# Output projection of a recurrent-attention block: eight block products against seven, on one core

## The chip, the core and the metric

The kernel runs on one core of a Trainium2 chip. The core has five engines that run side by side, each with a queue of its own: TensorE (PE in the profile; PEld is its weight load) multiplies matrices and writes its results into PSUM, VectorE (DVE) and ScalarE (ACT) do element by element work and can read PSUM, GpSimd (POOL) works on SBUF alone, and SyncE (SP) issues the DMAs. PSUM has eight banks of 512 float32 columns by 128 partitions.

The metric is the time of one execution in device microseconds. The kernel before takes 991.49 us (median of 3 runs, 991.46 to 991.51).

## The reference

There are B = 8 batches, H = 8 heads of D = 64, S = 512 tokens and Ns = 32 states in each batch. Tokens attend to states and states to tokens; the results are put one behind the other and go through a gated feed-forward block:

```python
scores = scale * np.matmul(x, state.transpose(0, 1, 3, 2))
a = softmax(scores)
xread = np.matmul(a, state)                      # (8, 8, 512, 64)
scores2 = scale * np.matmul(state, x.transpose(0, 1, 3, 2))
a2 = softmax(scores2)
sread = np.matmul(a2, x)                         # (8, 8, 32, 64)
x = concat([xread, sread]) -> (4352 tokens, 512)
xn = x / sqrt(mean(x * x) + 1e-06) * rms_g
g = xn @ w_gate                                  # 512 x 1536
val = xn @ w_val                                 # 512 x 1536
out = (g * sigmoid(g) * val) @ w_out             # 1536 x 512
```

(softmax and concat stand for the lines written out in the reference.) The feed-forward weights arrive as float64; the output is float32, 4352 x 512. The last line, the product with w_out, is what the change is about.

## The kernel before, in words

All matmuls are float32. One matmul of the source is two MATMUL instructions and two weight loads (LDWEIGHTS) in the trace. The stationary operand (lhsT) is 128 x 128, the moving operand (rhs) up to 512 columns wide.

*Start.* The weights are converted from float64 to float32 piece by piece on VectorE, GpSimd and ScalarE (lines 134 to 157): 24 pieces of w_gate and w_val into the tile w, 12 of w_out into the tile wo, in the order in which they are needed. The attention of batches 0 and 1 runs beside it.

*Batch loop* (lines 398 to 423). Batch b has two stages.

The **hidden stage** goes over m = 0 to 11, the twelve blocks of 128 of the 1536 hidden features. For every second m, make_v (lines 329 to 342) multiplies the states with the gate and value weights into v, which needs eight small matmuls (16 instructions, L335) and two ScalarE copies (L342). hidden (lines 344 to 360) then makes two 128 x 512 products in two PSUM banks, gp for the gate and vp for the value (two matmuls each, L350), and ScalarE takes a tanh of gp (L355). Two VectorE instructions make the hidden value h (L356, L358), 128 features by 512 tokens, in SBUF, from a pool of 14 buffers. Behind every m, between() puts two steps of the attention of batch b + 2 into the instruction stream, so that these are used up after the tenth m; in the projection between() has nothing left to issue, but in batch 0, where conversions may be left.

The **projection** (project, lines 362 to 372) goes over four blocks r of 128 tokens. For each it sums twelve matmuls, h of block m by wo of block m, 512 columns wide, in one PSUM bank (L367); ScalarE copies the bank to SBUF (L370) and SP issues the store of 128 x 512 (L377). make_v for the next batch's first two blocks stands right ahead of the projection.

*End.* Behind batch 7 the 256 state tokens of all batches go through the same two stages: hidden with w itself as the stationary operand and 256 columns (four matmuls per product, 192 instructions in all), and a projection of two blocks of 128 (48 instructions), each stored by four DMAs (L383).

PSUM: the pool fps has four banks and serves gp, vp and the projection (tile name f), in turn; aps and vps have two banks each, for the attention and for make_v. A bank comes free when its last reader is done.

The source gives the work in an order, but the framework fixes each engine's instruction order when it is built, by the source's order and by estimated times of what is ready, and places the semaphore waits.

Of the kernel before, what the change touches and what calls it, by code (L numbers as in the profile page):

```python
# [8 lines left out]
F32 = mybir.dt.float32  # L9
I32 = mybir.dt.int32  # L10
U32 = mybir.dt.uint32
ALU = mybir.AluOpType
# [4 lines left out]
P = 128  # L17
RAW_AHEAD = 4
# [4 lines left out]
def kernel(  # L23
# [103 lines left out]
    def ready(n):  # L127

        nonlocal n_ready
        while n_ready < min(n, len(pieces)):  # L130
            to_float32(n_ready)
            n_ready += 1

    def to_float32(k):


        load_piece(k + RAW_AHEAD)
        if k not in raw:
# [5 lines left out]
        top = two.tile([P, NI, P], I32, name="top")  # L144
        ex = two.tile([P, NI, P], I32, name="ex")
        man = two.tile([P, NI, P], F32, name="man")
# [14 lines left out]
    aT_s = {}  # L161
    xsT = consts.tile([P, NI, NT], F32, name="xsT")
# [146 lines left out]
    def state_norm():  # L309

        sq = one.tile([P, NI, NT], F32, name="sqT", tag="eS")
        SE.activation(out=sq, in_=xsT, func=ACTF.Square)
        sp = aps.tile([P, NT // P], F32, name="at")
        for r in range(NT // P):
            for i in range(NI):
                TE.matmul(out=sp[:, r:r + 1], lhsT=sq[:, i, P * r:P * r + P], rhs=ones[:, 0:1],
                          start=(i == 0), stop=(i == NI - 1))
        ss = two.tile([P, NT // P], F32, name="sst")
        VE.tensor_copy(ss, sp)
        rp = along(inverse_rms(ss, NT // P), NT // P)  # L320
# [8 lines left out]
    def make_v(b, mp):  # L329

        ready(4 * mp + 4)
        pv = [vps.tile([P, 4 * P], F32, name="pv") for e in range(2)]
        for j in range(4):
            for e in range(2):
                TE.matmul(out=pv[e][Ns * j:Ns * j + Ns, :],  # L335
                          lhsT=stT_g[b][D * e:D * e + D, j, :],
                          rhs=w[D * e:D * e + D, j, 2 * mp:2 * mp + 2].rearrange(
                              "p m k f -> p (m k f)"),
                          start=True, stop=True)
        v = v_sb[b, mp] = two.tile([P, 2, 2, 2, P], F32, name="v")  # L340
        for e in range(2):
            SE.copy(v[:, e].rearrange("p m k f -> p (m k f)"), pv[e])  # L342

    def hidden(m, n, lhs, rhs):

        gp = fps.tile([P, S], F32, name="f")
        vp = fps.tile([P, S], F32, name="f")
        for k, ps in enumerate((gp, vp)):
            for i, r in enumerate(rhs):
                TE.matmul(out=ps[:, 0:n], lhsT=lhs(i, k), rhs=r,  # L350
                          start=(i == 0), stop=(i == len(rhs) - 1))
        t = three.tile([P, S], F32, name="t", tag="t")
        h = hpool.tile([P, S], F32, name="h")

        SE.activation(out=t[:, 0:n], in_=gp[:, 0:n], func=ACTF.Tanh, scale=0.5)  # L355
        VE.scalar_tensor_tensor(out=t[:, 0:n], in0=t[:, 0:n], scalar=1.0, in1=gp[:, 0:n],  # L356
                                op0=ALU.add, op1=ALU.mult)
        VE.scalar_tensor_tensor(out=h[:, 0:n], in0=t[:, 0:n], scalar=0.5, in1=vp[:, 0:n],  # L358
                                op0=ALU.mult, op1=ALU.mult)
        return h  # L360

    def project(hh, n, store, between):
        ready(len(pieces))
        for r in range(n // P):
            op = fps.tile([P, DM], F32, name="f")
            for m in range(NM):
                TE.matmul(out=op, lhsT=hh[m][:, P * r:P * r + P], rhs=wo[:, m, :],  # L367
                          start=(m == 0), stop=(m == NM - 1))
            ot = three.tile([P, DM], F32, name="ot", tag="t")
            SE.copy(ot, op)  # L370
            store(r, ot)
            between()

    def store_tokens(b):
        def store(r, ot):
            r0 = T * b + P * r
            nc.sync.dma_start(out=out[r0:r0 + P, :], in_=ot)  # L377
        return store

    def store_states(r, ot):  # L380
        for j in range(4):
            r0 = T * (4 * r + j) + S
            nc.sync.dma_start(out=out[r0:r0 + Ns, :], in_=ot[Ns * j:Ns * j + Ns, :])  # L383

    done = object()
    for k in range(RAW_AHEAD):
        load_piece(k)
    load_state(1)
# [9 lines left out]
    for b in range(B):  # L398
        if b + LOOKAHEAD < B:
            steps = attention(b + LOOKAHEAD)  # L400
        elif b + LOOKAHEAD == B:
            steps = state_norm()
        else:
            steps = iter(())

        def between():
            for _ in range(2):
                next(steps, done)
                ready(n_ready + 1)

        hh = []
        for m in range(NM):
            if m % 2 == 0 and m + 2 < NM:
                make_v(b, m // 2 + 1)
            v = v_sb[b, m // 2]
            hh.append(hidden(m, S, lambda e, k: v[:, e, m % 2, k, :],
                             [aT_s[b][:, e, :] for e in range(2)]))
# [39 lines left out]
```

## Time and profile before

| what | value |
|---|---|
| median of 3 runs | 991.49 us |
| the profiled execution | 991.61 us |
| its span, first to last instruction | 989.6 us |
| mean granted TensorE clock | 0.971 |
| TensorE (PE) busy | 915.4 us, 3682 instructions |
| VectorE busy | 345.1 us |
| ScalarE busy | 226.3 us |
| GpSimd busy | 135.1 us |
| the projections' matmuls (L367) | 352.4 us, 816 instructions |
| the token hidden stages' matmuls (L350) | 357.6 us, 768 instructions |
| the states' hidden matmuls (L350) | 41.6 us, 192 instructions |

Engines overlap, so their busy times don't add up to the span. In a group of instructions, "busy" is the time in which at least one of the group runs, and the mean is that of one from start to end; TensorE starts an instruction before the one ahead of it has ended, so the mean of a matmul is longer than the distance between two of them. Times in a timeline or in the chain are microseconds from the start of the span. An arrow <- behind an idle time names what the engine waited for. "issue" is time in which an engine waited for nothing that the profile shows.

### The profile page before, as it was taken

To read this page: it belongs to the slowest core of one execution; us is meant where nothing else is said; L and a number is where in the kernel's file an instruction comes from. 1 tells how busy PE (TensorE), PEld (TensorE's weight loads), DVE (VectorE), ACT (ScalarE), POOL (GpSimd) and SP (SyncE) were. 2 spreads that over 40 slices of the span, in tenths; PEclk is the share of its full clock that TensorE was granted. 3 is DMA by queue.
4 is the path that set the end of the run, shared out by engine and by line. 5 is a ranking of instruction groups with operands and counts; after the bars stand their busy time and mean duration, and the time that the engine had idled before them with its cause. 6 is when DMAs were issued, how large, how long until landed. Compare 5 with 4: busy or idle time off the path is not lost.

```text
span 989.6 us, 9226 instructions
## 1 busy us (share of the span) xinstructions
PE 915.4 (93%) x3682; PEld 427.7 (43%) x3682; DVE 345.1 (35%) x533; ACT 226.3 (23%) x436; POOL 135.1 (14%) x169
## 2 busy tenths in 40 slices
PE   3487666999999999999999999999999999999998
PEld 2233323444444444444544454444444344344783
DVE  4899899402530153015300530054103300320120
ACT  3334233102420242014201430143102201210110
POOL 4766776100000000000000000001000000000000
PEclk9987787999999999999999999999999999999999
DMA  7463532200020002000200000000000000000000
GB/s 183 149 171 113 156 116 76 43 32 14 1 46 22 25 0 46 21 25 1 45 22 22 1 1 11 32 1 1 11 22 11 1 22 21 1 0 32 11 1 21
DMA packets 58363, 37.83 MB, mean 38 GB/s; under 512 B 40144, under 2 KB 52432, under 8 KB 58320
## 3 DMA queue, kind: packets, MB, share of 16 engines
q1 hardware_dynamic: 58320, 37.24, 13.2%
q8 instruction: 29, 0.48, 0.2%
q14 instruction: 14, 0.11, 0.0%
HBM read 28.31 MB, written 8.91 MB: 38 GB/s over the span
## 4 chain that ended last, share of the span: by engine, by line
PE 81%; DVE 10%; POOL 4%; issue 3%; SPq 1%; DMA 1%; ACT 0%; POOLq 0%; DVEq 0%
PE f L367 36%; PE f L350 35%; PE pv L335 4%; DVE ex L155 2%; PE at L271 2%; DVE top L152 2%; DVE man L153 2%; DVE ex L147 1%; POOL ex L150 1%; PE at L198 1%; POOL ex L149 1%; PE at L209 1%; PE at L177 1%; PE at L296 1%; DVE h L358 1%
## 5 line engine op out<-in xcount | busy, mean ns | idle before, releaser
L350 PE MATMUL f<-aT_s,v 128*128 128x512 f32 x768 | 357.6, 608 | 5.0 <-DVE t L356 4.4
L367 PE MATMUL f<-wo,h 128*128 128x512 f32 x816 | 352.4, 593 | 0.0
L356 DVE SCALAR_TENSOR_TENSOR t<-t,f 128x512 f32<-128x512 f32 (+1 forms) x108 | 70.9, 656 | 513.8 <-ACT t L355 513.8
L367 PEld LDWEIGHTS f<-wo,h 128*128 128x128 f32 x816 | 154.5, 190 | 197.3 <-issue 191.3
L350 PEld LDWEIGHTS f<-aT_s,v 128*128 128x128 f32 x768 | 140.2, 192 | 183.8 <-issue 152.1
L355 ACT ACTIVATE t<-f 128x512 f32<-128x512 f32 (+1 forms) x108 | 61.8, 572 | 201.4 <-PE f L350 189.7
L370 ACT COPY ot<-f 128x512 f32<-128x512 f32 x34 | 19.9, 586 | 331.8 <-PE f L367 331.8
L358 DVE SCALAR_TENSOR_TENSOR h<-t,f 128x512 f32<-128x512 f32 (+1 forms) x108 | 70.7, 654 | 47.4 <-PE f L350 47.1
L335 PE MATMUL pv<-w,stT_g 64*32 64x512 f32 x768 | 60.8, 609 | 9.2 <-POOL w L157 8.4
L342 ACT COPY v<-pv 128x512 f32<-128x512 f32 x96 | 51.7, 588 | 60.2 <-PE pv L335 59.8
L221 POOL TENSOR_SCALAR m<-m 128x2 f32<-128x2 f32 x8 | 2.8, 356 | 374.8 <-DVE m L218 374.8
L350 PE MATMUL f<-xsT,w 128*128 128x256 f32 x192 | 41.6, 379 | 0.0
L151 ACT ACTIVATE man<-raw 128x512 f32<-128x512 uint32 x36 | 24.5, 681 | 73.3 <-POOL w L157 44.9
L350 PEld LDWEIGHTS f<-xsT,w 128*128 128x128 f32 x192 | 36.5, 190 | 5.4 <-issue 0.5
L155 DVE SCALAR_TENSOR_TENSOR ex<-raw,ex 128x512 int32<-128x512 int32 x36 | 34.9, 969 | 5.9 <-POOL ex L150 5.9
L271 PE MATMUL at<-bd,aT 128*128 128x256 f32 x128 | 33.9, 410 | 1.4 <-ACT aT L263 0.7
L157 POOL TENSOR_TENSOR w<-man,ex 128x512 f32<-128x512 f32 x24 | 32.2, 1344 | 18.3 <-DVE ex L155 15.4
L271 PEld LDWEIGHTS at<-bd,aT 128*128 128x128 f32 x128 | 25.5, 204 | 15.2 <-issue 4.8
L149 POOL TENSOR_SCALAR ex<-ex 128x512 int32<-128x512 int32 x36 | 27.7, 769 | 24.5 <-DVE ex L147 23.4
L147 DVE TENSOR_SCALAR ex<-raw 128x512 int32<-128x512 int32 x36 | 28.9, 804 | 2.3 <-POOL w L157 2.3
L177 PE MATMUL at<-dg,ones 128*128 128x512 f32 (+1 forms) x18 | 12.0, 757 | 19.0 <-POOL dg L174 19.0
L153 DVE SCALAR_TENSOR_TENSOR man<-top,man 128x512 f32<-128x512 int32 x36 | 28.7, 798 | 0.4
(66 smaller groups left out, 442.0 us busy)
## 6 DMA issues: line engine op xcount, KB each, us to landing
x_b<-in_x_dram SPq DMA_DIRECT2D x32, 256.0 KB, 4.5
out_dram<-ot SPq DMA_DIRECT2D x32, 256.0 KB, 2.0
raw<-in_moe_w_gate_dram SPq DMA_DIRECT2D x12, 512.0 KB, 3.7
raw<-in_moe_w_val_dram SPq DMA_DIRECT2D x12, 512.0 KB, 3.6
raw<-in_moe_w_out_dram SPq DMA_DIRECT2D x12, 512.0 KB, 3.3
rows<-in_state_dram SPq DMA_DIRECT2D x32, 16.0 KB, 2.0
bd<-in_state_dram SPq DMA_DIRECT2D x32, 16.0 KB, 1.7
out_dram<-ot SPq DMA_DIRECT2D x8, 64.0 KB, 1.7
```

Source lines behind the costliest of these rows:

```text
L147: VE.tensor_scalar(ex, hi, 20, 0x7ff, op0=ALU.logical_shift_right, op1=ALU.bitwise_and)
L149: GE.tensor_scalar(ex, ex, 1151.0, 896.0, op0=ALU.min, op1=ALU.max)
L153: VE.scalar_tensor_tensor(out=man, in0=top, scalar=2.0 ** -20, in1=man, op0=ALU.mult, op1=ALU.add)
L155: VE.scalar_tensor_tensor(out=ex, in0=hi, scalar=-(1 << 31), in1=ex, op0=ALU.bitwise_and, op1=ALU.bitwise_or)
L271: TE.matmul(out=rp[:, e, :], lhsT=aT[:, e, c, :], rhs=bd[:, e].rearrange("p j d -> p (j d)"), start=True, stop=True)
L335: TE.matmul(out=pv[e][Ns * j:Ns * j + Ns, :], lhsT=stT_g[b][D * e:D * e + D, j, :], rhs=w[D * e:D * e + D, j, 2 * mp:2 * mp + 2].rearrange ...
L342: SE.copy(v[:, e].rearrange("p m k f -> p (m k f)"), pv[e])
L350: TE.matmul(out=ps[:, 0:n], lhsT=lhs(i, k), rhs=r, start=(i == 0), stop=(i == len(rhs) - 1))
L355: SE.activation(out=t[:, 0:n], in_=gp[:, 0:n], func=ACTF.Tanh, scale=0.5)
L356: VE.scalar_tensor_tensor(out=t[:, 0:n], in0=t[:, 0:n], scalar=1.0, in1=gp[:, 0:n], op0=ALU.add, op1=ALU.mult)
L358: VE.scalar_tensor_tensor(out=h[:, 0:n], in0=t[:, 0:n], scalar=0.5, in1=vp[:, 0:n], op0=ALU.mult, op1=ALU.mult)
L367: TE.matmul(out=op, lhsT=hh[m][:, P * r:P * r + P], rhs=wo[:, m, :], start=(m == 0), stop=(m == NM - 1))
```

## The change

The product with w_out is made by halves. For the tokens of a batch (n = 512, and n = 256 for the states) the hidden values h form a matrix of two token halves by two feature halves A(i, j) (i the token half, j the half of the twelve blocks m), and wo one of two feature halves by two output halves B(i, j). Instead of the eight products of half blocks, seven are made (the scheme of Strassen and Winograd), from sums of blocks:

- The hidden values are in one tile hb, 128 x 12 x 512, in place of the pool of 14 buffers. In batches 1 to 7 and for the states, hidden adds two VectorE instructions for m = 6 to 11: the sum s of two quarters of the hidden values (128 x 256) and a difference that overwrites the lower token half of block m - 6.
- weight_sums makes three matrices of weight sums (t1, t2, t4) and overwrites one quarter of wo, in twelve VectorE instructions of 128 x 512. They are put behind the first three m of batch 1.
- project_seven makes the seven products, each of R x 6 matmuls with 256 columns (R = 2 blocks of 128 rows, 1 for the states), in three banks: zs, xs and ys, each holding both row blocks side by side. Products 2, 3, 4 and 7 go into xs and products 1 and 6 into zs without clearing it in between, so that PSUM keeps the partial sums; product 5 goes into ys. In between, keep copies the sums so far to SBUF on ScalarE (p5 from zs, p1 and u2 and at the end c21 from xs), s is overwritten twice on VectorE (two instructions of 128 x 768 each time), and finish adds a kept copy to a bank on VectorE and stores the result as 128 x 256.
- Batch 0 keeps project as it was. Behind it the pools of the conversion (raws, and conv for its three intermediates) are closed, and the new tiles are put into their place.

```diff
-    raws = ctx.enter_context(tc.tile_pool(name="raws", bufs=RAW_AHEAD))
-    hpool = ctx.enter_context(tc.tile_pool(name="hpool", bufs=NM + 2))
...
+    early = ExitStack()
+    raws = early.enter_context(tc.tile_pool(name="raws", bufs=RAW_AHEAD))
+    conv = early.enter_context(tc.tile_pool(name="conv", bufs=2))
...
+    hb = consts.tile([P, NM, S], F32, name="hb")
...
-        h = hpool.tile([P, S], F32, name="h")
+        h = hb[:, m, :]
...
+        if seven and m >= HM:
+            k = m - HM
+            upper, lower = hb[:, k, 0:n // 2], hb[:, k, n // 2:n]
+            VE.tensor_tensor(out=seven["s"][:, k, 0:n // 2], in0=lower, in1=hb[:, m, n // 2:n],
+                             op=ALU.add)
+            VE.tensor_tensor(out=lower, in0=upper, in1=lower, op=ALU.subtract)
...
+    def weight_sums():
+        late = ctx.enter_context(tc.tile_pool(name="late", bufs=1))
+        seven["pool"] = ctx.enter_context(tc.tile_pool(name="halves", bufs=7))
+        seven["t"] = late.tile([P, 3, HM, HD], F32, name="wt")
+        seven["s"] = late.tile([P, HM, S // 2], F32, name="hs")
+        t1, t2, t4 = (seven["t"][:, i] for i in range(3))
+        for k in range(0, HM, 2):
+            def blk(i, j):
+                return wo[:, HM * i + k:HM * i + k + 2, HD * j:HD * j + HD]
+            for dst, a, b in ((t1[:, k:k + 2], blk(0, 1), blk(0, 0)),
+                              (t2[:, k:k + 2], blk(1, 1), t1[:, k:k + 2]),
+                              (blk(0, 1), blk(1, 1), blk(0, 1)),
+                              (t4[:, k:k + 2], blk(1, 0), t2[:, k:k + 2])):
+                VE.tensor_tensor(out=dst, in0=a, in1=b, op=ALU.subtract)
+            yield
+
+    def project_seven(n, store, between):
+        half = n // 2
+        R = half // P
+        t, s, pool = seven["t"], seven["s"], seven["pool"]
+        def product(ps, lhs, rhs, start):
+            for r in range(R):
+                for k in range(HM):
+                    TE.matmul(out=ps[:, r, :], lhsT=lhs(k)[:, P * r:P * r + P], rhs=rhs(k),
+                              start=(start and r == 0 and k == 0),
+                              stop=(k == HM - 1), skip_group_check=True)
...
+        def keep(ps):
+            kept = [pool.tile([P, HD], F32, name="ot2") for r in range(R)]
+            for r in range(R):
+                SE.copy(kept[r], ps[:, r, :])
+            return kept
+        def finish(kept, ps, i, j):
+            for r in range(R):
+                VE.tensor_tensor(out=kept[r], in0=kept[r], in1=ps[:, r, :], op=ALU.add)
+                store(R * i + r, HD * j, HD, kept[r])
...
+        zs = bank()
+        product(zs, S_, TS(0), True)
+        p5 = keep(zs)
+        for r in range(R):
+            c = slice(P * r, P * r + P)
+            VE.tensor_tensor(out=s[:, :, c], in0=s[:, :, c], in1=hb[:, 0:HM, c], op=ALU.subtract)
+        xs = bank()
+        product(xs, A(0, 0), B(0, 0), True)
+        p1 = keep(xs)
+        between()
+        product(xs, S_, TS(1), False)
+        u2 = keep(xs)
+        for r in range(R):
+            c = slice(P * r, P * r + P)
+            VE.tensor_tensor(out=s[:, :, c], in0=hb[:, HM:NM, c], in1=s[:, :, c], op=ALU.subtract)
+        between()
+        product(xs, A(1, 0), B(0, 1), False)
+        finish(p5, xs, 1, 1)
+        ys = bank()
+        product(ys, A(0, 1), B(1, 0), True)
+        finish(p1, ys, 0, 0)
+        between()
+        product(zs, S_, B(1, 1), False)
+        finish(u2, zs, 0, 1)
+        product(xs, A(1, 1), TS(2), False)
+        for r, c21 in enumerate(keep(xs)):
+            store(R + r, 0, HD, c21)
+        between()
...
         for m in range(NM):
...
             between()
+            next(sums, done)
         if b + 1 < B:
             make_v(b + 1, 0)
-        project(hh, S, store_tokens(b), between)
+        if b == 0:
+            ready(len(pieces))
+            early.close()
+            project(S, store_tokens(b), between)
+            sums = weight_sums()
+        else:
+            project_seven(S, store_tokens(b), between)
...
-    hh = [hidden(m, NT, lambda i, k: w[:, i, m, k, :], [xsT[:, i, :] for i in range(NI)])
-          for m in range(NM)]
-    project(hh, NT, store_states, lambda: None)
+    for m in range(NM):
+        hidden(m, NT, lambda i, k: w[:, i, m, k, :], [xsT[:, i, :] for i in range(NI)])
+    project_seven(NT, store_states, lambda: None)
```

More of the change, by code (lines that the diff above doesn't have):

```diff
@@ L143, in to_float32 @@
         lo = r.bitcast(U32).rearrange("p i (f two) -> p i f two", two=2)[:, :, :, 0]
-        top = two.tile([P, NI, P], I32, name="top")
-        ex = two.tile([P, NI, P], I32, name="ex")
-        man = two.tile([P, NI, P], F32, name="man")
+        top = conv.tile([P, NI, P], I32, name="top")
+        ex = conv.tile([P, NI, P], I32, name="ex")
+        man = conv.tile([P, NI, P], F32, name="man")
         VE.tensor_scalar(ex, hi, 20, 0x7ff, op0=ALU.logical_shift_right, op1=ALU.bitwise_and)
@@ L359, in hidden, with project @@
                                 op0=ALU.mult, op1=ALU.mult)
-        return h
-    def project(hh, n, store, between):
-        ready(len(pieces))
+        if seven and m >= HM:
[4 more added lines that the diff above has]
+            VE.tensor_tensor(out=lower, in0=upper, in1=lower, op=ALU.subtract)
+    def project(n, store, between):
         for r in range(n // P):
@@ L366, in project @@
             for m in range(NM):
-                TE.matmul(out=op, lhsT=hh[m][:, P * r:P * r + P], rhs=wo[:, m, :],
+                TE.matmul(out=op, lhsT=hb[:, m, P * r:P * r + P], rhs=wo[:, m, :],
                           start=(m == 0), stop=(m == NM - 1))
@@ L370, in project @@
             SE.copy(ot, op)
-            store(r, ot)
+            store(r, 0, DM, ot)
             between()
+    HM = NM // 2
+    HD = DM // 2
+    seven = {}
+    def weight_sums():
[13 more added lines that the diff above has]
+            yield
@@ new lines, in project_seven, with A, B, TS @@
+    def project_seven(n, store, between):
[8 more added lines that the diff above has]
+                              stop=(k == HM - 1), skip_group_check=True)
+        def A(i, j):
+            return lambda k: hb[:, HM * j + k, half * i:half * i + half]
+        def B(i, j):
+            return lambda k: wo[:, HM * i + k, HD * j:HD * j + HD]
+        def TS(i):
+            return lambda k: t[:, i, k, :]
+        def S_(k):
+            return s[:, k, 0:half]
+        def keep(ps):
[7 more added lines that the diff above has]
+                store(R * i + r, HD * j, HD, kept[r])
+        def bank():
+            return fps.tile([P, 2, HD], F32, name="f")
+        zs = bank()
[26 more added lines that the diff above has]
+        between()
@@ L374, in store_tokens, with store, store_states @@
     def store_tokens(b):
-        def store(r, ot):
+        def store(r, c0, n, ot):
             r0 = T * b + P * r
-            nc.sync.dma_start(out=out[r0:r0 + P, :], in_=ot)
+            nc.sync.dma_start(out=out[r0:r0 + P, c0:c0 + n], in_=ot)
         return store
-    def store_states(r, ot):
+    def store_states(r, c0, n, ot):
         for j in range(4):
             r0 = T * (4 * r + j) + S
-            nc.sync.dma_start(out=out[r0:r0 + Ns, :], in_=ot[Ns * j:Ns * j + Ns, :])
+            nc.sync.dma_start(out=out[r0:r0 + Ns, c0:c0 + n], in_=ot[Ns * j:Ns * j + Ns, :])
@@ L385 @@
     done = object()
+    sums = iter(())
     for k in range(RAW_AHEAD):
@@ L409, in between @@
                 ready(n_ready + 1)
-        hh = []
         for m in range(NM):
@@ L415 @@
             v = v_sb[b, m // 2]
-            hh.append(hidden(m, S, lambda e, k: v[:, e, m % 2, k, :],
-                             [aT_s[b][:, e, :] for e in range(2)]))
+            hidden(m, S, lambda e, k: v[:, e, m % 2, k, :],
+                   [aT_s[b][:, e, :] for e in range(2)])
             between()
+            next(sums, done)
         if b + 1 < B:
             make_v(b + 1, 0)
-        project(hh, S, store_tokens(b), between)
+        if b == 0:
[5 more added lines that the diff above has]
+            project_seven(S, store_tokens(b), between)
         for _ in steps:
             pass
-    hh = [hidden(m, NT, lambda i, k: w[:, i, m, k, :], [xsT[:, i, :] for i in range(NI)])
-          for m in range(NM)]
-    project(hh, NT, store_states, lambda: None)
+    for m in range(NM):
+        hidden(m, NT, lambda i, k: w[:, i, m, k, :], [xsT[:, i, :] for i in range(NI)])
+    project_seven(NT, store_states, lambda: None)
 _INS = ['x', 'state', 'moe_w_gate', 'moe_w_val', 'moe_w_out', 'moe_rms_g']
```

## The prediction, made before the changed kernel ran

> **What bounds the kernel now.** I read the page first, then stretches of the span engine by engine, then TensorE's waits, then the chain.
>
> ```profile
> span 989.6 us, 9226 instructions
> ...
> PE 915.4 (93%) x3682; PEld 427.7 (43%) x3682; DVE 345.1 (35%) x533; ACT 226.3 (23%) x436; POOL 135.1 (14%) x169
> ...
> PE   3487666999999999999999999999999999999998
> ```
>
> In the first eight slices TensorE (PE) waits; after that it never rests. The stretches (columns: microseconds, then busy time and instructions of each engine, granted clock, DMA) show a start of 189.4 us and, as one example each, a batch's projection and its hidden stage:
>
> ```profile
> 0.00:189.40 189.40, 120.31 (x629) 57.46 (x629) 158.97 (x231) 63.02 (x121) 118.40 (x136) 0.86 0.47 131
> ...
> 291.50:332.90 41.40, 41.40 (x104) 18.16 (x96) 0.00 (x0) 2.83 (x5) 0.00 (x0) 1.00 0.05 19
> 332.90:393.70 60.80, 60.80 (x334) 27.93 (x333) 28.22 (x45) 21.61 (x43) 3.03 (x6) 1.00 0.11 25
> ```
>
> TensorE's waits from 189 us to the end, all of them:
>
> ```profile
> PE at L261 <- DVE eS L253: 0.2, 1, 0.2
> PE at L177 <- POOL dg L174: 0.2, 1, 0.2
> ```
>
> So from 189 us on the time is the sum of TensorE's instructions at a granted clock of 1.00, and whatever shortens that stream shortens the kernel, unless it brings new waits. The chain prices the stages the change touches (start, duration, line, instructions):
>
> ```profile
> 291.59 41.40 PE f L367 x96
> ...
> 881.63 41.20 PE f L367 x96
> 922.83 41.44 PE f L350 x192
> 964.27 20.61 PE f L367 x48
> ```
>
> A float32 matmul of the source is two instructions: a projection has 4 row blocks x 12 = 48 matmuls and 96 instructions. One 128x512 instruction takes 41.40 / 96 = 0.431 us. The states' hidden stage (192 instructions) is the row I price everything by: it is made of 128x256 products with a new weight load each, which is what the change issues.
>
> ```profile
> L350 PE MATMUL f<-xsT,w 128*128 128x256 f32 x192 | 41.6, 379 | 0.0
> L350 PEld LDWEIGHTS f<-xsT,w 128*128 128x128 f32 x192 | 36.5, 190 | 5.4 <-issue 0.5
> L367 PEld LDWEIGHTS f<-wo,h 128*128 128x128 f32 x816 | 154.5, 190 | 197.3 <-issue 191.3
> ```
>
> There an instruction starts every 41.44 / 192 = 0.2158 us (379 ns is one instruction from start to modelled end; they overlap). Its weight load of 0.190 us is hidden, with 0.026 us to spare.
>
> **The change, part by part.** *TensorE's stream.* Seven products of 2 row blocks x 6 = 84 matmuls, 168 instructions, replace 96. 168 x 0.2158 = 36.25 us. Six batches save 41.40 - 36.25 = 5.15 each, batch 7 saves 41.20 - 36.25 = 4.95: 35.9 us. The states: 7 x 6 = 42 matmuls, 84 instructions, 18.13 us for 20.61: 2.5 us. Together **38.4 us**.
>
> *VectorE's sums.* They have no row of their own; these bracket them, with the 256 wide evaluation whose first operand or second lies in PSUM:
>
> ```profile
> L253 DVE TENSOR_TENSOR eS<-eS,z 128x1024 f32<-128x1024 f32 x8 | 9.7, 1214 | 0.0
> L190 DVE TENSOR_TENSOR stT_g<-stT,rms_g 128x128 f32<-128x128 f32 x8 | 2.2, 280 | 0.0
> L356 DVE SCALAR_TENSOR_TENSOR t<-t,f 128x256 f32<-128x256 f32 x12 | 5.1, 421 | 61.7 <-ACT t L355 61.7
> ```
>
> From 128 to 1024 elements that is 1.04 ns an element: 256 cost 0.41 us, 512 cost 0.68, 768 cost 0.95. Per batch: 12 sums of 256 in the hidden stage (4.9), four updates of s with 768 elements (3.8), six additions from PSUM (6 x 0.42 = 2.5): 11.2 us. VectorE has 28.2 us of work in a batch of 102.2 us (60.8 + 41.4), and none in the projection, so it ends near 39 of 97. In the half-stage m = 6 to 11 each step gains 0.82 us; TensorE's own four matmuls there are 8 x 0.43 = 3.4 us. I cost these at nothing; the cover is TensorE's 3.4 us and the second pair of PSUM banks. Without the cover they would cost up to 4.9 us a batch, 34 us over seven.
>
> *The weight sums,* once: 12 x 0.68 = 8.2 us, placed behind the first three steps of batch 1. Those steps:
>
> ```profile
> 231.80:247.10 15.30, 15.30 (x80) 6.80 (x73) 5.81 (x10) 5.11 (x9) 0.00 (x0) 1.00 0.07 22
> ```
>
> VectorE works 5.8 of their 15.3 us; it would be 14.0. Bounds: 0 (nine of the twelve only read wo, and VectorE is empty during the projection of batch 0) and 3 us (a step late by about 1 us, three times). I take 0.5.
>
> *The start of the projection.* Product 1 needs s of the last hidden step at its sixth matmul. Before it stand the eight small products for the next batch (1.0 us), then 5 x 0.43 us. After the last hidden product VectorE does the multiplication (0.69) and the sum (0.41): 1.1 us against 3.2. Hidden; were VectorE a further 2 us behind, TensorE would wait, and VectorE has no attention work by then.
>
> ```profile
> 290.50 1.09 PE L335 MATMUL pv<-w,stT_g 64*32 64x512 f32 x16
> 290.60 0.69 DVE L358 SCALAR_TENSOR_TENSOR h<-t,f 128x512 f32<-128x512 f32 x1 [0.40 <-PE f L350]
> ```
>
> *The updates of s.* Each starts when a product that reads s ends and takes 2 x 0.95 us; the next reader of s stands a whole product (24 x 0.2158 = 5.2 us, 2.6 for the states) later. Hidden.
>
> *The kept copies.* This is the one new wait. Products 2, 3 and 4 run in one bank, xs; after 2 and after 3 ScalarE copies both halves of it before TensorE adds on. Nothing in the trace reads half a bank while the other half is written, so I bound it. If a wait concerns a half alone, the first half's copy runs under the second half's 1.3 us of matmuls and the second's under the first half of the next product: 0. If it concerns the bank, the stream stops for the whole exchange:
>
> ```profile
> 90.01 0.57 ACT L263 COPY aT<-at 128x512 f32<-128x512 f32 x1
> ...
> 90.63 4.63 PE L271 MATMUL at<-bd,aT 128*128 128x256 f32 x10 [0.72 <-ACT aT L263]
> ...
> 231.93 1.07 ACT L342 COPY v<-pv 128x512 f32<-128x512 f32 x2 [0.44 <-PE pv L335]
> ...
> 291.52 14.86 PE L367 MATMUL f<-wo,h 128*128 128x512 f32 x34
> ...
> 302.12 0.59 ACT L370 COPY ot<-f 128x512 f32<-128x512 f32 x1 [9.37 <-PE f L367]
> ```
>
> ```profile
> L355 ACT ACTIVATE t<-f 128x256 f32<-128x256 f32 x12 | 4.6, 384 | 34.9 <-PE f L350 34.9
> ```
>
> The copy at 302.12 starts 0.26 us after the 24 instructions that began at 291.52 have run out (291.52 + 24 x 0.431 = 301.86). Two copies of 512 take 1.07 us where one takes 0.59, so the second adds 0.48; two of 256 then take about 0.38 + 0.27 = 0.65. TensorE follows 0.05 us after a copy's end (90.58 to 90.63). Sum 1.0 us, up to 1.2 with a weight load (0.19) that could not be pulled ahead; 0.7 to 0.9 for the states, which have one copy. Fully exposed: 14 x 1.1 + 2 x 0.8 = 17 us.
>
> The Trainium skill (PSUM — Partial Sum Buffer, "PSUM bank collisions raise a hardware error") says that two engines may not touch one bank in the same quadrant at once, whatever columns they use, and that one guards by bank. By it the wait is the bank's. No row here tests it; the sum would lie on the 17 us side but for what follows.
>
> What fills the gap is product 5. It writes another bank (ys) and needs only hidden values and weights that are final. The instruction order isn't the source's: where TensorE's next work was not ready, other ready work was set in front of it, one source matmul at a time.
>
> ```profile
> 51.97 0.68 DVE L289 COPY e2T<-at 128x512 f32<-128x512 f32 x1
> ...
> 52.41 1.91 PE L350 MATMUL f<-aT_s,v 128*128 128x512 f32 x2
> ...
> 54.26 1.08 PE L296 MATMUL at<-x_b,e2T 128*32 128x64 f32 x32
> ...
> 60.12 0.30 PE L187 MATMUL at<-ident,rows 128*128 128x128 f32 x1
> ```
>
> The first hidden product of batch 0 (L350) stands between attention(0)'s transposes and their reader L296, and ahead of attention(1)'s first instruction (L187 at 60.12), which the source has before it. Three matmuls of product 5 (3 x 0.43 = 1.3 us) cover one exchange and twelve are there for two. The order is fixed beforehand by estimated times, so a rest remains; the waits of 0.2 us above are such rests. I take 0.15 us for each of 16 exchanges: 2.4 us.
>
> *Copies, stores, end.* ScalarE has 8 copies of 256 (3.1 us) for 4 of 512 (2.4) a batch, in a stretch where it works 2.8 of 41.4 us. SP issues 8 stores for 4 a batch, and 16 for 8 at the states, four per tile; four small issues take 1.75 us, less than a 2.6 us product, so the last tile does not queue. The last copy shrinks from 0.59 to 0.38: -0.2 us.
>
> ```profile
> 235.62 1.75 SPq L80 DMA_DIRECT2D rows<-in_state_dram  x4
> ...
> 984.90 0.59 ACT L370 COPY ot<-f 128x512 f32<-128x512 f32 x1 [9.71 <-PE f L367]
> ```
>
> *Hidden values in one buffer.* Steps 0 to 5 of the next batch overwrite what product 4 read last, steps 6 to 11 what product 7 read six steps earlier: no wait. The fourth bank and zs, free one product before the end, serve the next batch's first step.
>
> The **sum** against the profiled execution (991.6 us, span 989.6; the median is 991.49, so nothing is to be converted): 991.6 - 38.4 - 0.2 + 2.4 + 0.5 = 955.9; I say **956**.
>
> **The rivals.** *The exchanges stay exposed* (the order is not changed, or changed by too little): 991.6 - 38.6 + 17 + 0.5 = 970.5. For it: no row rules out a wait for the whole bank, and the order comes from estimates. Against: the hoisted L350.
>
> *The half-width stream doesn't hold its pace,* and the kernel gets slower. One mechanism: the weight loads, now one for every 256 columns, no longer hide. The decisive pace is 41.40 / 168 = 0.246 us; the 0.026 us of slack in the row of the states is thin, and a load wholly exposed makes 0.190 + 0.216 = 0.406 us, 68.2 us a batch and 34.1 for the states: 7 x 26.8 + 13.5 = +201 us, 1193 us; at 0.265 us, the mean of
>
> ```profile
> L271 PE MATMUL at<-bd,aT 128*128 128x256 f32 x128 | 33.9, 410 | 1.4 <-ACT aT L263 0.7
> ```
>
> (33.9 / 128), it is 7 x 3.1 + 1.7 = +23, 1015 us. Against: that row holds short bursts, each with its own tail, and the slow start; 192 pairs in a row ran at 0.2158. The Trainium skill (TensorE: Matmul & The Clock Gate, "Part 3: Packing small matmuls") has loads overlap running matmuls only for other row groups, which would give the 0.406; the trace disagrees, with 192 loads of 0.190 and 192 matmuls in 41.44 us.
>
> *VectorE becomes the bound in the hidden stage,* so that the gain goes into its added work: 991.6 - 38.6 + 34 = 987, from the cover above being gone. Against: 28 us busy of 61. I count it for little.
>
> **How the numbers follow.** Forecast 956 (exchanges filled or not needed): 0.68. Exposed, wholly or half (963 to 971): 0.23. VectorE: 0.03. Slower weight loads: 0.05. Something that leaves no change: 0.01. Low end: all costs at zero, 991.6 - 38.6 = 953, and 1.5 us for a start that is ordered anew. High end: exposed, 971. Outside is about 0.15. A measurement of this kernel tells a change from none at about 0.2%, 2 us: faster 0.93, same 0.02, slower 0.05.
>
> **What would show it.** The group of 128x256 matmuls of the projection with 7 x 168 + 84 = 1260 instructions and a pace near 0.216 us; 96 instructions of 128x512 left (batch 0); matmuls of ys between those of xs; TensorE's waits for ScalarE's copies near 2 us in all (17 if exposed); VectorE busy 345 + 90 us. Wrong would be a pace above 0.23, waits behind VectorE's sums in batches 1 to 7, or a start other than 189 us.

## The result, and the profile after

The changed kernel takes **956.49 us** (median of 4 runs, 956.26 to 956.93) against 991.50 us for the kernel before on the same chip: a ratio of 0.9647, 95% interval 0.963 to 0.9664, 35 us less. The forecast was 956. The profiled execution after took 956.26 us, its span 954.4.

The page of the changed kernel, the lines that answer to those shown of before:

```profile
span 954.4 us, 10638 instructions
...
PE 878.3 (92%) x4222; PEld 527.5 (55%) x4222; DVE 436.2 (46%) x716; ACT 227.7 (24%) x466; POOL 135.2 (14%) x169
...
PE   4476576799999999999999999999999999999998
```

TensorE is full from the ninth slice on (191 us), before from the eighth (173 us); there is less of its stream. VectorE has 91 us more work and nothing shows of it. The chain, the work that ended last followed back in time, gives the stages (start, duration, line, instructions):

```profile
189.81 41.40 PE f L375 x96
291.97 36.74 PE f L414 x168
...
853.70 36.54 PE f L414 x168
890.24 41.44 PE f L353 x192
931.68 18.14 PE f L414 x84
```

Batch 0 keeps its 41.40 us. Batches 1 to 6 take 36.74 instead of 41.40 and batch 7 36.54 instead of 41.20, 4.66 us less each and 32.6 in all; the states take 18.14 instead of 20.61, 2.5 us less. The hidden stage of the states is 41.44 us in both. So the whole 35 us is in the projections.

TensorE's timeline of batch 1's projection shows how the seven products ran (start, duration to the modelled end, line, tiles, count):

```profile
290.88 1.09 PE L338 MATMUL pv<-w,stT_g 64*32 64x512 f32 x16
291.90 5.45 PE L414 MATMUL f<-wt,hs 128*128 128x256 f32 x24
297.18 6.21 PE L414 MATMUL f<-wo,hb 128*128 128x256 f32 x28
303.26 5.45 PE L414 MATMUL f<-wt,hs 128*128 128x256 f32 x24
308.55 9.80 PE L414 MATMUL f<-wo,hb 128*128 128x256 f32 x44
318.18 5.34 PE L414 MATMUL f<-wo,hs 128*128 128x256 f32 x24
323.36 5.34 PE L414 MATMUL f<-wt,hb 128*128 128x256 f32 x24
328.64 1.09 PE L338 MATMUL pv<-w,stT_g 64*32 64x512 f32 x16
```

A product is 24 instructions. Behind product 2 stand 28: four belong to product 5 and were set there while ScalarE copies xs. Behind product 3 (303.26) stand 44: four more of product 5, the 24 of product 4, and the last 16 of product 5. That is the filling that the prediction argued for. What the other engines do meanwhile:

```profile
294.79 0.96 DVE L450 TENSOR_TENSOR hs<-hs,hb 128x768 f32<-128x768 f32 x1 [2.20 <-PE f L414]
...
297.38 0.65 ACT L434 COPY ot<-f 128x256 f32<-128x256 f32 x2 [4.25 <-PE f L414]
297.38 0.96 DVE L450 TENSOR_TENSOR hs<-hs,hb 128x768 f32<-128x768 f32 x1 [1.63 <-PE f L414]
302.56 0.65 ACT L434 COPY ot<-f 128x256 f32<-128x256 f32 x2 [4.53 <-PE f L414]
```

VectorE's first update of s starts at 294.79, when the first row block of product 1 is done: for s, in SBUF, the wait is for the part. ScalarE's two copies from PSUM come one behind the other from 297.38 on, when the whole product is done, though the first needs only the first row block: in PSUM the wait is for both halves. The two from 302.56 take 0.65 us, as priced, and product 3 follows at 303.26.

### The profile page after: what moved, and what is told of

Its sections match the earlier page's. It is cut to its first block, busy times and chain, and to the rows that moved or that the text cites. A ratio compares the mean times of both kernels' runs of the same rounds, so it can differ in the third digit from the quotient of the medians.

```text
span 954.4 us, 10638 instructions
## 1 busy us (share of the span) xinstructions
PE 878.3 (92%) x4222; PEld 527.5 (55%) x4222; DVE 436.2 (46%) x716; ACT 227.7 (24%) x466; POOL 135.2 (14%) x169
## 4 chain that ended last, share of the span: by engine, by line
PE 82%; DVE 9%; POOL 4%; issue 3%; DMA 1%; ACT 1%; SPq 1%; POOLq 0%; DVEq 0%; ACTq 0%
PE f L353 36%; PE f L414 29%; PE pv L338 5%; PE f L375 4%; PE at L274 2%; DVE ex L158 2%; DVE top L155 1%; DVE man L156 1%; DVE ex L150 1%; PE at L201 1%; DMA x_b<-in_x_dram 1%; PE at L212 1%; POOL ex L153 1%; PE at L299 1%; POOL ex L152 1%
## 5 line engine op out<-in xcount | busy, mean ns | idle before, releaser
L414 PE MATMUL f<-wo,hb 128*128 128x256 f32 x540 | 120.1, 380 | 0.0
L414 PEld LDWEIGHTS f<-wo,hb 128*128 128x128 f32 x540 | 102.0, 190 | 15.5 <-ACT ot L434 1.9
L361 DVE SCALAR_TENSOR_TENSOR hb<-t,f 128x512 f32<-128x512 f32 (+1 forms) x108 | 70.6, 654 | 47.0 <-PE f L353 46.9
L414 PE MATMUL f<-wt,hs 128*128 128x256 f32 x360 | 81.7, 383 | 0.0
L434 ACT COPY ot<-f 128x256 f32<-128x256 f32 x60 | 19.6, 375 | 256.0 <-PE f L414 256.0
L414 PEld LDWEIGHTS f<-wt,hs 128*128 128x128 f32 x360 | 67.3, 190 | 16.0 <-DVE hb L361 5.0
L439 DVE TENSOR_TENSOR ot<-ot,f 128x256 f32<-128x256 f32 x45 | 17.1, 418 | 92.1 <-PE f L414 49.3
L375 PE MATMUL f<-wo,hb 128*128 128x512 f32 x96 | 41.5, 593 | 0.0
L414 PE MATMUL f<-wo,hs 128*128 128x256 f32 x180 | 40.2, 379 | 0.0
L414 PE MATMUL f<-wt,hb 128*128 128x256 f32 x180 | 40.2, 379 | 0.0
```

The source lines that it names most:

```text
L375: TE.matmul(out=op, lhsT=hb[:, m, P * r:P * r + P], rhs=wo[:, m, :], start=(m == 0), stop=(m == NM - 1))
L414: TE.matmul(out=ps[:, r, :], lhsT=lhs(k)[:, P * r:P * r + P], rhs=rhs(k), start=(start and r == 0 and k == 0), stop=(k == HM - 1), skip_gr ...
L434: SE.copy(kept[r], ps[:, r, :])
```

## The experiments

The changed kernel took 956.49 us in its first runs and 956.82 in a later one; the kernel before took 991.42 to 991.69 us beside the runs below.

Theory: the gain is TensorE's shorter stream at the pace of the states' hidden stage; the new waits, at the exchanges with ScalarE, are waits for a whole PSUM bank, and they hardly show because product 5 fills them. An exchange is the stretch in which ScalarE copies a bank that TensorE will add to; it is open when TensorE has nothing to do in it. Rivals: there is no such wait; or the half width, VectorE's sums or the place of the sums cost something of their own that hides in the total.

### The half width alone

The kernel before with each projection matmul of 512 columns made as two of 256; eight products of half blocks, no sums.

```diff
-            for m in range(NM):
-                TE.matmul(out=op, lhsT=hh[m][:, P * r:P * r + P], rhs=wo[:, m, :],
-                          start=(m == 0), stop=(m == NM - 1))
+            for c in (0, DM // 2):
+                for m in range(NM):
+                    TE.matmul(out=op[:, c:c + DM // 2], lhsT=hh[m][:, P * r:P * r + P],
+                              rhs=wo[:, m, c:c + DM // 2], start=(c == 0 and m == 0),
+                              stop=(m == NM - 1), skip_group_check=True)
```

> The kernel before, with every projection matmul of 512 columns made as two of 256 (eight products of half blocks, nothing else changed): twice the weight loads and twice the instructions. Theory (half width costs nothing by itself): 192 instructions x 0.2158 = 41.4 us for a batch as before, 991 to 993.5 us (up to 0.25 us a projection for starts). Rival (loads not hidden): at 0.246 us an instruction 47.2 us for a batch and +44 us, 1035.

Measured: 993.41 us, ratio to before 1.002 (1.0011 to 1.0029). The groups of the projection in this run:

```profile
L368 PE MATMUL f<-wo,h 128*128 128x256 f32 x1632 | 354.4, 379 | 0.0
L368 PEld LDWEIGHTS f<-wo,h 128*128 128x128 f32 x1632 | 309.5, 190 | 48.1 <-DVE h L358 5.9 <-issue 0.5
```

1632 loads of 0.190 us behind matmuls that start every 354.4 / 1632 = 0.217 us: twice the loads stay hidden. The stage took 352.4 us before. The width costs 2 us and the eighth product's absence is the gain. The line of the Trainium skill that stood behind the slower rival (TensorE: Matmul & The Clock Gate, "Part 3: Packing small matmuls", loads overlap matmuls in flight only where the row group differs) does not hold for these full 128x128 loads. The same Part says ahead of that line that a load is also pulled ahead when it goes to the background weight buffer; the 0.217 us here agree with that.

### The order of the products

The changed kernel with TensorE's instructions held to the source's order from the first seven-product projection on. The edge fixes the order of issue and adds no wait.

```diff
+    def _queue(self, i):
+        i = getattr(i, "ins", i)
+        if self.on:
+            if self.last is not None:
+                self.tc.add_manual_dep(i, self.last.name, mybir.DependencyInfo(
+                    mybir.DependencyClass.NoSync, mybir.DependencyReason.DATA), reason="order")
+            self.last = i
...
     def project_seven(n, store, between):
+        TE.on = True
```

> The changed kernel with TensorE held to the source's order from the first seven-product projection on (order alone, no new wait), so that product 5 can no longer be set into the gaps. My theory (a wait for the whole bank at each of the 16 exchanges, filled by product 5 in the changed kernel): each exchange now stops the matmuls for about 0.9 to 1.0 us in batches 1 to 7 (in the changed kernel 0.65 for two copies, 0.2 ahead of them and 0.05 behind) and about 0.65 for the states, so 14 x 0.95 + 2 x 0.65 = 14.6 us more than the changed kernel: 970 to 972 us. Rival (a wait for the half that is written next, hidden without any filling): within 1 us of the changed kernel's 956.5.

Measured: 990.39 us (988.12 to 997.94), ratio to before 1.0006 (0.9984 to 1.0029): the whole gain is gone, 18 to 20 us more than the 970 to 972 expected. TensorE's waits in it from 185 us on:

```profile
PE f L35 <- ACT ot L454: 11.2, 16, 0.7
PE at L38 <- DVE eS L275: 11.1, 4, 2.8
PE at L35 <- POOL dg L196: 2.0, 1, 2.0
PE at L38 <- DVE sr L323: 1.7, 4, 0.4
PE at L35 <- DVE e2T L311: 1.4, 4, 0.4
```

The first line is what was looked for, 16 exchanges (14 for the tokens, 2 for the states). The rest, 16.2 us, are waits in the hidden stages, for attention: there too the order had been rearranged, and my edit undid that. The total could not tell the two apart, so I narrowed the edit to the projections: the same chain inside a projection, which ends here, and all that comes later is only kept behind the projection's last instruction.

```diff
...
             store(R + r, 0, HD, c21)
+        TE.on = False
         between()
```

> The first run held the hidden stages to the source's order too, and TensorE waited there as well (16 us behind attention's sums). Here the order is the source's inside the seven-product projections alone; nothing later may be set in front of a projection's end, all else is free as in the changed kernel. The trace of the first run shows 0.90 us from the end of a product to the start of the next at an exchange and 38.47 us for a projection (36.74 in the changed kernel). Theory (the bank's wait, filled by product 5 in the changed kernel): 7 x 1.73 + 2 x 0.6 for the states = 13.3 us more than the changed kernel, 969 to 971 us. Rival (what the filling hides is small, the first run lost its time elsewhere): 957 to 960.

Measured: **970.32 us**, ratio 0.9786 (0.9772 to 0.9801), 13.8 us more than the changed kernel, and near the total that the prediction gave its rival of open exchanges (970.5). Its waits and batch 1's products 2 to 5:

```profile
PE f L36 <- ACT ot L455: 11.2, 16, 0.7
PE at L36 <- POOL dg L197: 0.2, 1, 0.2
```

```profile
297.98 5.34 PE L36 MATMUL f<-wo,hb 128*128 128x256 f32 x24
304.06 5.45 PE L36 MATMUL f<-wt,hs 128*128 128x256 f32 x24 [0.74 <-ACT ot L455]
310.24 10.63 PE L36 MATMUL f<-wo,hb 128*128 128x256 f32 x48 [0.74 <-ACT ot L455]
```

Product 3 starts 6.08 us after product 2, where 24 instructions last 5.18: 0.90 us open. A projection takes 38.47 us in this run and in the one before it (330.50 - 292.03 there), so the other 20 us of that run lie outside the projections, where its trace shows the 16.2 us of waits for attention.

### The bank

The same order, with xs in two banks, one for each row block, each half used.

```diff
...
+        def banks():
+            return [fps.tile([P, 2, HD], F32, name="f")[:, 0, :] for r in range(R)]
...
-        xs = bank()
+        xs = banks()
```

> The same order with xs in two banks, one for each row block. Theory (the wait is the bank's): no stop at the exchanges of batches 1 to 7, a projection of 36.46 us as in the second run, the two exchanges of the states open: 956.5 - 7 x 0.28 + 1.2 = 955.7 us, within 1 us. Rival (the stop comes from the order or from ScalarE being late): 969 or more.

Measured: **956.29 us**, ratio 0.9644 (0.9628 to 0.966). Nothing is set into the gaps and there are no gaps:

```profile
297.59 5.34 PE L36 MATMUL f<-wo,hb 128*128 128x256 f32 x24
302.77 5.34 PE L36 MATMUL f<-wt,hs 128*128 128x256 f32 x24
307.95 10.52 PE L36 MATMUL f<-wo,hb 128*128 128x256 f32 x48
```

Only the two exchanges of the states, which have one row block, are left open (0.9 us of waits in all). A projection takes 36.46 us instead of 38.47, so an open exchange costs 1.0 us, its gap of 0.90 and 0.1 behind it. So the wait concerns both halves of the bank together, not the half that is read. The Trainium skill (PSUM — Partial Sum Buffer, "PSUM bank collisions raise a hardware error") says that one guards PSUM by bank, and the waits that the framework set here do so. In this kernel a bank is also one tile, so these runs do not tell whether the framework goes by the bank or by the tile; what the chip would do without the wait was not run. The same edit had first been made with everything held to the source's order:

> As the run in source order, but xs is two banks, one for each row block, half of each used. If the wait is the bank's, the copy of the first row block now runs under the second's matmuls and the second's under the first of the next product, and the exchanges of batches 1 to 7 vanish without any filling; those of the states (one row block) stay, 2 x 0.65 = 1.3 us: 956 to 959 us. If the stop has another cause (the order itself, ScalarE late, the sums on VectorE) it stays near the run in source order, 970 us.

It gave 980.21 us, ratio 0.9887 (0.9873 to 0.9902): the exchanges had vanished, the waits for attention in the hidden stages were still there. The expected 956 to 959 had overlooked them, as in the first run.

With the order free and two banks:

> The changed kernel with xs in two banks, order free. Theory: 956.5 - 7 x 0.28 = 954.5 us, within 0.5; the exchanges of the states stay filled by product 5. Rival: 956.5, as with the projections held to the source's order in two banks (956.3, whose states were not filled).

Measured: 954.89 us, ratio 0.9631 (0.9618 to 0.9644), beside

> The changed kernel itself once more, on the chip of these runs: 956.5 us, within 0.5.

which gave 956.82 us on the same chip (0.9651, 0.9638 to 0.9664). The two banks are worth 1.9 us: a projection takes 36.46 us instead of 36.74 (in batch 7 36.26 instead of 36.54), so a filled exchange had still cost 0.14 us.

### VectorE's cover

The changed kernel with more work on VectorE behind each of the steps m = 6 to 11: first two, then six more differences of 128x256, written to a spare tile that nothing reads. The first run's edit (the second has range(6)):

```diff
             VE.tensor_tensor(out=lower, in0=upper, in1=lower, op=ALU.subtract)
+            for _ in range(2):
+                spare = seven["pool2"].tile([P, S // 2], F32, name="spare")
+                VE.tensor_tensor(out=spare[:, 0:n // 2], in0=upper, in1=lower, op=ALU.subtract)
```

> The changed kernel with two more VectorE differences of 128x256 (into a spare tile, never read) behind the two sums of each step m = 6 to 11, so twice the added VectorE work of the hidden stage. Theory (the sums lie in TensorE's shadow: a step is 3.45 us of matmuls, VectorE has 1.37 + 0.84 us in it, and 0.84 more fits): within 1 us of the changed kernel, 956 to 957.5 us. Rival (VectorE is already close to the bound): 7 x 6 x 0.84 = 35 us more at most, at least 5.

> The same with six more differences, eight in a step. VectorE's step is then 1.37 + 8 x 0.42 = 4.7 us at most (less where one starts before the last has ended) against TensorE's 3.45. Theory: the cover is a step's matmuls plus one step of lead from the second pair of banks, so it breaks here: 6 x 1.3 = 7.6 us of lateness a batch less 3.4 of lead, 0 to 4 us a batch, 957 to 985 us, with TensorE waiting for the tile of the sums or for a bank. Rival (VectorE's sums never reach TensorE): 956.5.

Measured: 956.74 us (ratio 0.9648, 0.9634 to 0.9663) and 957.20 us (0.9653, 0.9639 to 0.9668), with no wait of TensorE for VectorE in either. Twice the sums are free, as expected. Four times are nearly so, at the low end of what I gave, but that run proves little, since a spare difference can be put off. So the sum s itself was written seven times, product 1 needing the last:

```diff
-            VE.tensor_tensor(out=seven["s"][:, k, 0:n // 2], in0=lower, in1=hb[:, m, n // 2:n],
-                             op=ALU.add)
+            for _ in range(7):
+                VE.tensor_tensor(out=seven["s"][:, k, 0:n // 2], in0=lower,
+                                 in1=hb[:, m, n // 2:n], op=ALU.add)
```

> In the runs with more differences the spare ones could be put off, since nothing needs them. Here the sum s itself is written seven times (eight VectorE instructions in a step m = 6 to 11), and product 1 needs the last. VectorE's step becomes 1.3 + 8 x 0.34 to 0.46 = 4.0 to 5.0 us against 3.45 of TensorE: 3 to 9 us late when the projection starts. Theory (product 2, 5.2 us, and product 5 go first, so that VectorE's lateness is covered once more): within 4 us of the changed kernel, 956.5 to 960. Rival (product 1's wait is open): 7 x 3 to 9 = 21 to 63 us more.

Measured: 963.31 us (0.9716, 0.9703 to 0.973), 6.5 more than the changed kernel on that chip. Neither expectation holds: more than 4, far less than 21. The waits, and the start of batch 1's projection:

```profile
PE f L415 <- DVE hs L368: 3.6, 8, 0.6
...
```

```profile
292.20 2.51 PE L415 MATMUL f<-wt,hs 128*128 128x256 f32 x10
294.55 1.46 PE L415 MATMUL f<-wo,hb 128*128 128x256 f32 x6
296.40 3.29 PE L415 MATMUL f<-wt,hs 128*128 128x256 f32 x14 [0.39 <-DVE hs L368]
299.53 4.91 PE L415 MATMUL f<-wo,hb 128*128 128x256 f32 x22
```

Product 2 was set in front of the rest of product 1, but only three of its matmuls (six instructions), which is too little by 0.39 us. These waits are 3.6 of the 6.5 us; batch 1's projection takes 329.69 - 292.20 = 37.49 us instead of 36.74, 0.75 more, of which the 0.39 is the part that stands as a wait. What makes up the rest stays open. VectorE was less late than priced, too:

```profile
292.20 2.10 DVE L368 TENSOR_TENSOR hs<-hb 128x256 f32<-128x256 f32 x6
```

Six in 2.10 us: one follows another after about 0.34 us, though each lasts 0.42. The cover holds for the change's own sums with room, and gives way by 0.75 us in batch 1 at four times the work.

### Batch 0 too

With the weight sums made ahead of batch 0's projection, its eight products can be seven.

```diff
...
-            next(sums, done)
...
-            project(S, store_tokens(b), between)
             sums = weight_sums()
-        else:
-            project_seven(S, store_tokens(b), between)
+            next(sums)
+            for k in range(HM):
+                sum_of(k, S)
+            for _ in sums:
+                pass
+            for k in range(HM):
+                difference_of(k, S)
+        project_seven(S, store_tokens(b), between)
```

sum_of and difference_of are the two VectorE instructions that hidden adds in the other batches.

> The seven products in batch 0 too. The weight sums (12 x 0.68 us) and the sums of batch 0 (12 x 0.41) run on VectorE behind its hidden stage, 13 us, of which product 1 needs the first 4.5; products 2 and 5 need none of them and are 10.4 us of matmuls that can go first. Theory: the projection of batch 0 takes 36.7 to 38 us in place of 41.4, so 952 to 954 us. Rival (TensorE waits for VectorE's sums, because VectorE is still behind with the conversions at 190 us): 956 or more.

Measured: 952.84 us, ratio 0.9615 (0.9599 to 0.9631). VectorE's sums are covered but for one short wait:

```profile
190.24 1.99 PE L418 MATMUL f<-wt,hs 128*128 128x256 f32 x8
192.07 1.03 PE L418 MATMUL f<-wo,hb 128*128 128x256 f32 x4
193.41 3.72 PE L418 MATMUL f<-wt,hs 128*128 128x256 f32 x16 [0.32 <-DVE wt L405]
196.97 5.34 PE L418 MATMUL f<-wo,hb 128*128 128x256 f32 x24
...
227.56 1.09 PE L338 MATMUL pv<-w,stT_g 64*32 64x512 f32 x16
```

The projection takes 227.56 - 190.24 = 37.3 us instead of 41.4, with one wait of 0.32 us for the weight sums. Both edits together:

> The seven products in batch 0 too, and xs in two banks in all batches, order free. The run with batch 0 alone gave 952.84 us. Theory: the two banks take the exchanges away, so a projection falls from 36.74 to 36.46 us, 8 x 0.28 = 2.2 us: 950.6 us, within 0.7. Rival (the filled exchanges cost nothing, the 0.28 us is the order's): 952.5 to 953.

Measured: **950.64 us**, ratio 0.9589 (0.9576 to 0.9602): faster than both kernels, 2.2 us below the run with batch 0 alone, as the 8 x 0.28 us foresaw.

## Why the prediction was right

*TensorE's stream sets the time.* Right. The 35 us of the result are 32.6 in seven projections and 2.5 in the states.

*The pace.* Right: the 24 instructions of a product that stands between two others take 5.18 us, 0.2158 each. Over the forecast 540 + 360 + 180 + 180 = 1260 instructions of 128x256 the trace has 6 x 36.74 + 36.54 + 18.14 = 275.1 us, 0.218 each.

*The saving of a projection.* Taken 0.2 us too large in six batches, 1.2 us in all. Batches 1 to 6 have a make_v right ahead of the projection and one right behind it; batch 7 has none. The projection of batch 7 is 0.20 us shorter than the others before (41.20 for 41.40) and after (36.54 for 36.74), and with two banks its 36.26 us are the bare 168 x 0.2158 = 36.25. The 0.2 us stand at the two ends. Behind make_v, product 1 of batch 1 takes 297.18 - 291.90 = 5.28 us, and its last product 328.64 - 323.36 = 5.28 to the next make_v. In batch 7 product 1 takes 5.18:

```profile
853.53 5.34 PE L414 MATMUL f<-wt,hs 128*128 128x256 f32 x24
858.71 6.21 PE L414 MATMUL f<-wo,hb 128*128 128x256 f32 x28
```

The prediction set 41.40, which holds this 0.2 us, against 36.25, which does not, and so got 5.15; without exchanges all seven save the 4.95 that it gave batch 7. The seven projections save 4.66 each, 4.95 less two filled exchanges of 0.14.

*The exchanges.* The price, the wait for the bank and the filling are each shown: 1.0 us open (1.0 to 1.2 had been given), none with two banks, and 0.14 us left of a filled one where I had put 0.15, a guess from the 0.2 us waits of before. The profile lists none of it as a wait of TensorE for ScalarE, where I had said that about 2 us would be listed; it shows as weight loads that start late (last section). The open rival's total of 970.5 us was met by the run that took the filling away (970.32), with some luck: its exchanges were taken 0.1 us too dear each and its saving 1.2 us too large.

*VectorE's sums at nothing.* Right, with 91 us of added work for a forecast of about 90. The margin is larger than I had worked out, because an instruction's mean duration isn't its distance to the next one.

*The weight sums.* They cost nothing in batch 1, where I had put 0.5 us. They were not there: VectorE did nine of the twelve from 182 us on, three in batch 0's projection,

```profile
L401 DVE TENSOR_TENSOR wt<-wo,wt x6: 673/680/693, 183.1 to 190.3; 128x512 f32<-128x512 f32 x6
L401 DVE TENSOR_TENSOR wt<-wo x3: 677/679/681, 182.3 to 186.9; 128x512 f32<-128x512 f32 x3
L401 DVE TENSOR_TENSOR wo<-wo x3: 691/691/692, 222.7 to 226.1; 128x512 f32<-128x512 f32 x3
```

(the row's three times are the shortest, the median and the longest duration in ns; then first and last start). Batch 0's projection began 0.4 us later than before, 189.8 for 189.4. The other nine traces with early weight sums and the old projection in batch 0 have it between 189.9 and 190.6, the one other without such sums (half width alone) at 189.1. So the start is later by 0.4 to 1.5 us in the changed kernel's family, where the prediction had it unchanged; whether the early sums are the cause was not tried.

*The end.* The last copy took 0.37 us for 0.59, as forecast.

*The other rivals.* Weight loads that don't hide are ruled out by the run with half width alone. VectorE as the bound is ruled out by twice its sums.

So the mechanism was right, and that the total agrees to half a microsecond is in part luck, since small terms offset each other. Against the forecast went 1.2 us of saving that was not there and 0.4 us at the start. For it went 0.5 us for weight sums in batch 1 that did not come, 0.3 us for the states' exchanges (18.14 us for the 18.13 of the bare products), 0.1 us at the exchanges of the tokens (14 x 0.14 for 14 x 0.15) and 0.2 us that the kernel before lost at a wait the changed one does not have. That leaves 0.5 us, where the profiled 956.26 is 0.4 above the sum of 955.9.

## What to carry to other kernels

Where one engine's stream sets the time, price a change by the nearest stage that already has the new shape at full pace, here 128x256 products with a load each, and not by a short burst of it. Take the stage that it replaces in the same way: 41.40 us held 0.2 us of its neighbours, and the batch without neighbours showed it. A partial sum that stays in PSUM while another engine reads it stops TensorE for a whole exchange, 1.0 us here, as the framework sets the waits; give each part that is read alone its own bank, or have work for another bank ready and ready early. Before holding an order by hand to test something, look whether the order does other work as well: here that was worth about 20 us in a stage that the test was not about.

## What the runs showed of the hardware that I had not expected

*A filled exchange still costs about 0.1 us where the copy ends too late for the weight load.* The weight loads in the changed kernel, batch 1:

```profile
303.26 5.05 PEld L414 LDWEIGHTS f<-wt,hs 128*128 128x128 f32 x24 [0.27 <-ACT ot L434]
...
317.97 5.15 PEld L414 LDWEIGHTS f<-wo,hs 128*128 128x128 f32 x24
```

Product 6's first load (317.97) runs 0.21 us ahead of its matmul at 318.18, under the product before. Product 3's load starts with the product, at 303.26, behind the copy that ends at 302.56 + 0.65 = 303.21. Product 3 lasts 5.29 us to the next start, product 6 5.18. In the states' projection the same four instructions fill the exchange, but there is one copy only:

```profile
936.89 0.37 ACT L434 COPY ot<-f 128x256 f32<-128x256 f32 x1 [2.22 <-PE f L414]
937.34 2.56 PEld L414 LDWEIGHTS f<-wt,hs 128*128 128x128 f32 x12
937.56 2.75 PE L414 MATMUL f<-wt,hs 128*128 128x256 f32 x12
940.15 4.48 PE L414 MATMUL f<-wo,hb 128*128 128x256 f32 x20
```

The copy ends at 937.26, the load runs 0.22 us ahead of its matmul, and the product takes 2.59 us, the bare 12 x 0.2158. So a filling of a few tenths of a microsecond more should take the rest away too. That the late load is the cause is read from these rows and was not tried by itself.

*VectorE's 128x256 instructions follow each other at 0.34 us with a duration of 0.42 each* (six in 2.10 us, above), so a sum of durations, 2.53 us, overstates VectorE's time by a fifth. The same holds for ScalarE's two copies: 0.65 us for two of 0.37.
